# A transformer block on one core: DMA transposes and later transfers in the lead-in

## The chip, the cores and the metric

The kernel runs on one core of one Trainium2 chip. The metric is device time in microseconds (us) of one execution. Engines are called as in the profile: PE (matmuls; PEld is its weight load), DVE (vector), ACT (activations), POOL (GpSimd) and SP, which here only issues DMAs.

## The reference

A pre-norm transformer block in bf16, with 2048 rows of width 1024, 32 heads of 32 channels and an FFN width of 3584:

```
qkv = layernorm(x) @ wqkv                      # 1024 x 3072
o   = softmax(q k^T / sqrt(32)) v, per head
h   = x + o @ wo
out = h + gelu(layernorm(h) @ w1 + b1) @ w2 + b2
```

## The kernel before

**Order of the work.** The program is written as a graph of tasks, one per instruction or per small group, with an engine, a cost, a priority and the buffers that they read and write. `Graph.schedule` (L109) runs a list scheduler over it when the program is built and so fixes each engine's order; on the chip every engine works through its list in order and waits on semaphores. PE's choice among ready tasks is `pick_pe` (L1171): scores (kind "qk") first; then softmax times V ("pv") and row sums ("den") once enough rounds wait; then filler ("bg": projections, FFN), the lowest program number first. SP takes the lowest priority number first. Filler needs a PSUM bank: `slot()` (L518) hands out banks 6 and 7 alone, and the task that copies the result out gives the bank back. An attention job (one block of 256 queries of one head group) holds one of these banks from its first pv to the copies L866 and L873 in `finish`. Banks 0 to 5 hold scores, as three units of two banks.

**Attention.** A head group is 4 heads, 128 channels. A job has 8 rounds of 256 keys. A round is 8 score matmuls (`qk`, L784), two exponentials on ACT (L795, written to one of NR = 9 PT slots, and in the lead-in also to the extra slots PX that lie over buffers not yet in use), 8 pv matmuls (L821), an addition of the two key halves on DVE (L836, three buffers PS) and 4 matmuls with ones for the row sums (L850).

**Lead-in** (L1015 to L1087). The sixteen x tiles (128 rows each) are loaded into 8 buffers `xrb`. `lead_norm(hc)` (L1031) normalises two tiles into `xb` (4 buffers; statistics L598 and L613 on DVE, roots on POOL) and transposes both by 8 PE matmuls each (L619) into a shared bank, from which ACT (tiles 0 to 3) or DVE (the others, L628) copies to `xnT`. Each half `hc` of 256 rows then gives K of group 0 (`proj_half`, copied out by L758), the first three also Q, and three jobs (NLJ = 3) of group 0 start their score rounds on these halves: 24 rounds in all. V of a single head group (`proj_v1`, copied out by L740) comes from whole or strip matmuls: `mm(..., narrow)` makes either one 128-wide matmul (L549, L552) or four matmuls of 32 output rows (L546). `merge_tiles` (L210) turns runs of strip tasks back into whole ones where they stand alone or fill 3 us. The jobs' pv may start only when `gate`, the last copy of group 0's V, is done. After the lead-in come, for each group g, its Q and K projections (`proj`, copied out by L669), V, and the attention of query blocks 0 and 1, with 2 too for g = 1 and 2; the later query blocks run beside output projection and FFN. For those, `xnT` of rows 512 to 2047 is copied to DRAM (`xd`, three DMAs of 1 MB) in `lead_norm` and read back at about 258 us. Weights of groups 1 and up are loaded by `rest_w`, all after the load of x tile 15. In the FFN stage `ln2` transposes by DMA (L575) on SP's queue.

Of the kernel before, what the change touches and what calls it, by code (L numbers as in the profile page):

```python
# [12 lines left out]
P = 128  # L13
# [315 lines left out]
def build_kernel(nc, A_x, A_wqkv, A_wo, B_w1, B_b1, B_w2, B_b2, out):  # L329
# [98 lines left out]
    NXB = 4  # L428
# [106 lines left out]
    def drop(t, bank):  # L535
        if isinstance(bank, Slot):
            t.rel = bank

    def mm(bank, lhsT, rhs, start, stop, reads, narrow, cols=(0, 512), after=()):

        c0, c1 = cols
        occ = MM * (c1 - c0) / 512.0 + 0.0026
        if narrow:
            fns = []
            for j in range(4):
                fns.append(lambda p, j=j: p.matmul(psum[32 * j:32 * j + 32, bi(bank), c0:c1], lhsT[:, 32 * j:32 * j + 32], rhs,  # L546
                                                   start=start, stop=stop, tile_position=(0, 32 * j), skip_group_check=True))
            t = pe(fns, occ, reads=reads, writes=[bb(bank)], mode="col", after=after)
            t.whole = lambda p: p.matmul(psum[:, bi(bank), c0:c1], lhsT, rhs, start=start, stop=stop,  # L549
                                         skip_group_check=True)  # L550
# [99 lines left out]
    def proj(which, g, tc, bank, evac, direct=False):  # L650

        blk, c = divmod(which * D + g * P, 512)
        for dc in range(DC):
            mm(bank, Wall[blk][:, dc, c:c + P], xnT[:, tc, dc, :], dc == 0, dc == DC - 1,
               [B_W[blk][c // P]] + B_xnTt[tc], True)
        if which == 1:
            dst, wr = KT[:, g, 512 * tc:512 * tc + 512], B_KT[8 * g + 2 * tc:8 * g + 2 * tc + 2]
        elif direct:
            n = q_slot(0, g, 2)
            q_slots[1, g] = n + 1  # L660
            dst, wr = QT[:, n:n + 2, :].rearrange("p a c -> p (a c)"), B_QT[n:n + 2]
        else:
            s = cnt["sg"] % NSG
            cnt["sg"] += 1
            dst, wr = stg[:, s, :], [B_stg[s]]
        if evac == "act":
            t = act(lambda a: a.activation(dst, psum[:, bi(bank), :], ACT.Copy), 512, reads=[bb(bank)], writes=wr, prio=-1)
        else:
            t = dve(lambda v: v.tensor_copy(dst, psum[:, bi(bank), :]), c_dve_ps(512), reads=[bb(bank)], writes=wr)  # L669
# [92 lines left out]
    class Att:  # L762
# [8 lines left out]
        def qk(self, job, r, s=None):  # L771


            qb, g = job
            qs = q_slots[qb, g]
            us = [self.unit % self.n_units, (self.unit + 1) % self.n_units]
            self.unit += 2
            fns, banks = [], []
            for i in range(2):
                for h in range(4):  # L780
                    k0 = (2 * r + i) * P

                    def fn(p, i=i, h=h, k0=k0):
                        return p.matmul(psum[:, 2 * us[h // 2] + h % 2, 256 * i:256 * i + 256],  # L784
                                        KT[32 * h:32 * h + 32, g, k0:k0 + P], QT[32 * h:32 * h + 32, qs, :],
                                        start=True, stop=True, tile_position=(32 * h, 0))
                    fns.append(fn)
            for u in us:
                banks += [B_ps[2 * u], B_ps[2 * u + 1]]
            pe(fns, 0.222, reads=[B_KT[8 * g + r], B_QT[qs]], writes=banks, kind="qk", mode="row")  # L790
            if s is None:
                s = self.rounds % NR
                self.rounds += 1
            for k, u in enumerate(us):
                act(lambda a, u=u, k=k: a.activation(PTs[s][:, k, :, :], psum[:, 2 * u:2 * u + 2, :], ACT.Exp, bias=0.0, scale=SCALE),  # L795
                    1024, reads=[B_ps[2 * u], B_ps[2 * u + 1]], writes=[B_PTs[s][k]], kind="exp")
            return s
# [86 lines left out]
    pending = []  # L884

    def attention_round(job, r, lag=1):
        s = att.qk((job.qb, job.g), r)
        pending.append((job, r, s))
        attention_drain(lag)

# [155 lines left out]
    lead_rounds = []  # L1046
    lead_norm(0)
    for hc in range(8):
        ev = "act" if hc == 0 else "dve"
        if hc < NLJ:  # L1050
            proj_half(0, hc, slot(), ev)
        proj_half(1, hc, slot(), ev)
        if hc < 7:
            lead_norm(hc + 1)
        for k, r in [(k, hc) for k in range(min(hc, NLJ))] + ([(hc, r) for r in range(hc + 1)] if hc < NLJ else []):
            n = 8 * k + r
            s = NR + 15 if n == 0 else n - 1 if n < 9 else n
            lead_rounds.append((k, r, att.qk((k, 0), r, s)))
    att.rounds = 8
    hold = [t for t in gr.tasks if t.eng == E.DVE][-1:]  # L1060
    for c in range(4):
        proj_v1(4 * c, 0, 4, slot(), "dve", 0, True)
    gate = gr.tasks[-1]
    for k in range(NLJ):
        job = Job(k, 0, slot(2))
        for _, r, s in [x for x in lead_rounds if x[0] == k]:
            job.pv(r, s)
    pool_banks = {6: [t for t in gr.tasks if t.kind == "warm"][-1:], 7: []}
    lx = last_x[-1:]

    def rest_w(blk, c0, c1):
        load_w(blk, -3, c0, c1, after=lx)
# [84 lines left out]
    def ready_rounds(now):  # L1157
# [120 lines left out]
```

## Time and profile before

| | |
|---|---|
| median of 3 runs | 1090.35 us (1087.95 to 1093.55) |
| the profiled execution | 1091.97 us, its span 1090.2 us |
| mean granted PE clock | 0.994 |
| busy over the span | PE 96%, ACT 93%, DVE 69%, POOL 4%, DMA engines 54.1% |
| first 100 us, busy | PE 89.3, ACT 80.9, DVE 79.0 us |
| 100 to 200 us, busy | PE 99.1, ACT 100.0, DVE 63.5 us |
| 1000 to 1090.2 us, busy | PE 85.1, ACT 41.2, DVE 20.8 us |

The span is the time between the first and the last instruction that the profiler saw. A row of a timeline gives start, duration, engine, line, operation, output and inputs, and in brackets how long the engine was idle before it and which instruction released it. Times of stages are counted from the start of the span.

### The profile page before, as it was taken

Reading aid. Unit: us, or ns where it says so; the run is one execution under the profiler, and the core shown is the slowest. Engines: PE = TensorE matmul, PEld = TensorE weight load, DVE = VectorE, ACT = ScalarE, POOL = GpSimd, SP = SyncE. Lnnn points to the kernel's source line nnn. Section 1 sums busy time; section 2 is a strip of 40 time slices with the busy share of each in tenths; the row PEclk is TensorE's granted clock in tenths of the full one; section 3 lists DMA queues with packets and bytes.
Section 4 is the critical chain, followed back from the end, with each engine's and each line's share of the span. In section 5 each row is a group of like instructions: output and inputs, shape, how many; then the busy total and the mean of one; then the engine's idle time right before and its main releaser. Section 6 shows DMA issues by size and latency. Waiting matters only on the chain.

```text
span 1090.2 us, 41817 instructions
## 1 busy us (share of the span) xinstructions
PE 1045.6 (96%) x19048; PEld 609.6 (56%) x19107; DVE 755.9 (69%) x1453; ACT 1014.5 (93%) x1116; POOL 43.4 (4%) x110
## 2 busy tenths in 40 slices
PE   8989999998899999999999999999999999999998
PEld 6656555554344664574475457446545754474483
DVE  7886666666576896599489659948974967696401
ACT  4989999999999999999999999999999999999650
POOL 3200000000010001001000100100010000000100
PEclk9999999999999999999999999999999999899999
DMA  7640010008464667665685766567586656987370
GB/s 194 199 123 11 14 41 3 2 3 287 142 167 133 183 180 209 210 189 154 209 251 157 220 215 189 155 217 233 142 239 205 182 179 160 308 236 228 96 246 20
DMA packets 280146, 178.03 MB, mean 163 GB/s; under 512 B 42656, under 2 KB 274976, under 8 KB 279200
## 3 DMA queue, kind: packets, MB, share of 16 engines
q1 hardware_dynamic: 279968, 175.35, 54.1%
q8 instruction: 150, 2.46, 0.9%
q14 instruction: 28, 0.23, 0.1%
HBM read 161.16 MB, written 10.49 MB: 157 GB/s over the span
## 4 chain that ended last, share of the span: by engine, by line
PE 54%; ACT 39%; DVE 5%; issue 1%; DMA 1%; SPq 0%; POOL 0%; POOLq 0%; DVEq 0%
ACT PT L795 35%; PE ps L549 18%; PE ps L546 12%; PE ps L784 8%; PE ps L821 6%; PE ps L552 5%; PE ps L850 3%; ACT PX L795 2%; DVE PS L836 2%; ACT uu L983 2%; DMA xrb<-in_A_x_dram 0%; DVE OD L866 0%; PE ps L1025 0%; SPq L570 0%; DVE OD L873 0%
## 5 line engine op out<-in xcount | busy, mean ns | idle before, releaser
L795 ACT ACTIVATE PT<-ps 128x1024 bf16<-128x1024 f32 x992 | 922.4, 1082 | 14.7 <-PE ps L784 14.3
L836 DVE TENSOR_TENSOR PS<-PT 128x1024 bf16<-128x1024 bf16 x434 | 286.6, 685 | 128.9 <-PE ps L850 68.1
L784 PE MATMUL ps<-QT,KT 32*128 32x256 bf16 x4096 | 205.3, 274 | 10.7 <-ACT PT L795 5.4
L821 PE MATMUL ps<-PT,V 128*32 128x256 bf16 x3968 | 174.4, 274 | 2.8 <-ACT PT L795 2.8
L784 PEld LDWEIGHTS ps<-QT,KT 32*128 32x128 bf16 x4096 | 61.2, 92 | 166.3 <-ACT PT L795 134.8
L850 PE MATMUL ps<-PS,ones 128*32 128x256 bf16 x1792 | 124.6, 275 | 4.8 <-DVE PS L836 4.0
L821 PEld LDWEIGHTS ps<-PT,V 128*32 128x32 bf16 x3968 | 102.1, 97 | 29.4 <-issue 6.8
L549 PE MATMUL ps<-hnT,a_w1r 128*128 128x256 bf16 x949 | 116.5, 274 | 1.1 <-DVE gT L961 0.5
L549 PEld LDWEIGHTS ps<-hnT,a_w1r 128*128 128x128 bf16 x949 | 87.9, 98 | 25.8 <-issue 14.5
L546 PE MATMUL ps<-a_w2r,gT 128*32 128x512 bf16 x1372 | 98.3, 381 | 0.4 <-DVE hch L1007 0.2
L549 PE MATMUL ps<-a_w2r,gT 128*128 128x512 bf16 x382 | 93.8, 380 | 4.2 <-issue 2.9
L546 PE MATMUL ps<-hnT,a_w1r 128*32 128x256 bf16 x2476 | 88.9, 274 | 4.0 <-issue 1.6
L961 DVE TENSOR_TENSOR gT<-ps,b1f 128x512 bf16<-128x512 f32 x98 | 67.2, 686 | 17.5 <-PE ps L546 9.3
L546 PEld LDWEIGHTS ps<-hnT,a_w1r 128*32 128x32 bf16 x2476 | 60.4, 96 | 20.6 <-issue 16.8
L1007 DVE SCALAR_TENSOR_TENSOR hch<-ps,hch 128x512 bf16<-128x512 f32 x32 | 21.9, 685 | 69.9 <-PE ps L552 47.1
L850 PEld LDWEIGHTS ps<-PS,ones 128*32 128x32 bf16 x1792 | 47.0, 96 | 30.7 <-DVE PS L836 14.2
L549 PEld LDWEIGHTS ps<-a_w2r,gT 128*128 128x128 bf16 x413 | 35.2, 98 | 47.4 <-issue 13.4
L549 PE MATMUL ps<-xnT,Wall 128*128 128x512 bf16 (+1 forms) x256 | 53.5, 344 | 4.5 <-DVE rr L876 2.8
L983 ACT ACTIVATE uu<-uu 128x1024 bf16<-128x1024 bf16 x49 | 53.9, 1108 | 0.0
L546 PEld LDWEIGHTS ps<-a_w2r,gT 128*32 128x32 bf16 x1372 | 30.0, 96 | 25.6 <-issue 14.0
L603 POOL CAST mvb<-mv 128x2 bf16<-128x2 f32 (+1 forms) x25 | 4.9, 201 | 987.2 <-DVE mv L600 987.2
L549 PE MATMUL ps<-Wall,xnT 128*128 128x128 bf16 (+1 forms) x443 | 43.9, 247 | 0.0
(89 smaller groups left out, 1007.9 us busy)
## 6 DMA issues: line engine op xcount, KB each, us to landing
a_w2r<-in_B_w_dram SPq DMA_DIRECT2D x105, 512.0 KB, 5.7
a_w1r<-in_B_w_dram SPq DMA_DIRECT2D x98, 512.0 KB, 4.4
a_w1r<-in_A_wo_dram SPq DMA_DIRECT2D x32, 512.0 KB, 4.2
b_w1r<-in_B_w_dram SPq DMA_DIRECT2D x14, 512.0 KB, 6.1
a_w1r<-in_A_wqkv_dram SPq DMA_DIRECT2D x11, 512.0 KB, 5.0
Wall<-in_A_wqkv_dram SPq DMA_DIRECT2D x17, 256.0 KB, 4.7
xrb<-in_A_x_dram SPq DMA_DIRECT2D x16, 256.0 KB, 4.0
hch<-in_A_x_dram SPq DMA_DIRECT2D x16, 256.0 KB, 5.2
```

The lines of the kernel that those rows point to most:

```text
L546: fns.append(lambda p, j=j: p.matmul(psum[32 * j:32 * j + 32, bi(bank), c0:c1], lhsT[:, 32 * j:32 * j + 32], rhs, start=start, stop=stop, ...
L549: t.whole = lambda p: p.matmul(psum[:, bi(bank), c0:c1], lhsT, rhs, start=start, stop=stop, skip_group_check=True)
L552: t = pe(lambda p: p.matmul(psum[:, bi(bank), c0:c1], lhsT, rhs, start=start, stop=stop), occ, reads=reads, writes=[bb(bank)], mode="full" ...
L603: pool(lambda g: g.tensor_copy(mvb[:, sl, :], mv_l[:, sl, :]), 0.25, reads=B_mv[sl], writes=B_mvb[sl], prio=prio)
L784: return p.matmul(psum[:, 2 * us[h // 2] + h % 2, 256 * i:256 * i + 256], KT[32 * h:32 * h + 32, g, k0:k0 + P], QT[32 * h:32 * h + 32, qs, :],
L795: act(lambda a, u=u, k=k: a.activation(PTs[s][:, k, :, :], psum[:, 2 * u:2 * u + 2, :], ACT.Exp, bias=0.0, scale=SCALE), 1024, reads=[B_ps ...
L821: fns.append(lambda p, i=i, h=h: p.matmul(psum[32 * h:32 * h + 32, bi(bank), 0:256], V[:, g, 2 * r + i, 32 * h:32 * h + 32], PTs[s][:, h / ...
L836: dve(lambda v: v.tensor_tensor(PS[:, n, :, :], pairs[:, :, 0:256], pairs[:, :, 256:512], ALU.add), c_dve(1024, 2), reads=B_PTs[s], writes ...
L850: fns.append(lambda p, h=h, rhs=rhs, i=i: p.matmul(psum[32 * h:32 * h + 32, bi(bank), 256:512], ones32[:, :], rhs, start=False, stop=last, ...
L961: t = dve(lambda v: v.tensor_tensor(g[:, fc:fc + 2, :], psum[:, bi(bank), :].rearrange("p (f c) -> p f c", f=2), b1f[:, fc:fc + 2].unsquee ...
L983: act(lambda a: a.activation(w, w, ACT.Tanh, bias=0.0, scale=KT2), 1024, reads=[B_uu[i]], writes=[B_uu[i]], prio=-1)
L1007: drop(dve(lambda v, hs=hs, bank=bank, half=half: v.scalar_tensor_tensor(hch[:, hs, c], psum[:, bi(bank), :], half, hch[:, hs, c], ALU.mul ...
```

## The change

- x tiles 10 to 15 are transposed by DMA (`dma_transpose`, from `xb` straight into `xnT`) instead of by PE, PSUM and a DVE copy.
- V of groups 0 and 1 is asked for as whole matmuls (`narrow` left at False).
- `gate` is now two tasks, the last K half of group 0 and the last V copy of group 0. All matmul groups that are started after K of group 1 (`late`) wait for it, where before only V of group 1 did.
- Group 1's weights wait for x tile 11 instead of 15; all later weights wait for the transpose of tile 15.
- The copies of `xnT` to DRAM stand in the program after the lead-in and group 1's weights; their priority is as before.
- A Q projection that goes through the staging buffer `stg` waits for a free one before its first matmul rather than before its copy.
- The lead-in's jobs are made earlier and handed to `qk`; the order of the program is otherwise the same.

```
 def mm(bank, lhsT, rhs, start, stop, reads, narrow, cols=(0, 512), after=()):
+    after = list(after) + (late if start else [])
...
 def proj(which, g, tc, bank, evac, direct=False):
+    o = B_stg[cnt["sg"] % NSG]
+    free = o.w + o.r if which == 0 and not direct else []
...
+               [B_W[blk][c // P]] + B_xnTt[tc], True, after=free if dc == 0 else ())
...
+LEAD_PE = 10
+last_t = []
...
     for tt in tts:
-        tr_tile(tt, slot(), "act" if tt in LEAD_ACT else "dve")
+        if tt < LEAD_PE:
+            tr_tile(tt, slot(), "act" if tt in LEAD_ACT else "dve")
+        else:
+            tc, t4 = divmod(tt, 4)
+            last_t[:] = [dma_transpose(xnT[:, tc, :, t4 * P:(t4 + 1) * P], xb[:, tt % NXB, :], P * 2048, [B_xb[tt % NXB]], [B_xnTt[tc][t4]], -4)]
...
-    if hc in (3, 5, 7):
-        tc = hc // 2
-        dma(xd[tc - 1], xnT[:, tc, :, :], P * 8192, reads=B_xnTt[tc], writes=[B_xd[tc - 1]], prio=1)
...
     proj_half(1, hc, slot(), ev)
+    lead_k = gr.tasks[-1]
...
 for c in range(4):
-    proj_v1(4 * c, 0, 4, slot(), "dve", 0, True)
-gate = gr.tasks[-1]
+    proj_v1(4 * c, 0, 4, slot(), "dve")
+gate = [lead_k, gr.tasks[-1]]
...
-lx = last_x[-1:]
+lx = last_x[3:4]
...
 rest_w(WK, P, 2 * P)
 rest_w(WQ, P, 2 * P)
 rest_w(WV, P, 4 * P)
+lx = last_t or last_x[-1:]
+for tc in range(1, 4):
+    dma(xd[tc - 1], xnT[:, tc, :, :], P * 8192, reads=B_xnTt[tc], writes=[B_xd[tc - 1]], prio=1)
...
     for tc in range(4):
         proj(1, g, tc, slot(), "dve")
+    late[:] = gate
     if g == 1:
         for c in range(4):
-            proj_v1(4 * c, 1, 4, slot(), "dve", 0, True, [gate])
+            proj_v1(4 * c, 1, 4, slot(), "dve")
...
-    if gate.done is None or gate.done > now + 1e-9:
+    if any(x.done is None or x.done > now + 1e-9 for x in gate):
```

More of the change, by code (lines that the diff above doesn't have):

```diff
@@ L537, in drop @@
             t.rel = bank
+    late = []
     def mm(bank, lhsT, rhs, start, stop, reads, narrow, cols=(0, 512), after=()):
+        after = list(after) + (late if start else [])
         c0, c1 = cols
@@ L652, in proj @@
         blk, c = divmod(which * D + g * P, 512)
+        o = B_stg[cnt["sg"] % NSG]
+        free = o.w + o.r if which == 0 and not direct else []
         for dc in range(DC):
             mm(bank, Wall[blk][:, dc, c:c + P], xnT[:, tc, dc, :], dc == 0, dc == DC - 1,
-               [B_W[blk][c // P]] + B_xnTt[tc], True)
+               [B_W[blk][c // P]] + B_xnTt[tc], True, after=free if dc == 0 else ())
         if which == 1:
@@ L771, in qk @@
         def qk(self, job, r, s=None):
-            qb, g = job
+            qb, g = job.qb, job.g
             qs = q_slots[qb, g]
@@ L886, in attention_round @@
     def attention_round(job, r, lag=1):
-        s = att.qk((job.qb, job.g), r)
+        s = att.qk(job, r)
         pending.append((job, r, s))
@@ L1038, in lead_norm @@
         for tt in tts:
-            tr_tile(tt, slot(), "act" if tt in LEAD_ACT else "dve")
+            if tt < LEAD_PE:
[3 more added lines that the diff above has]
+                last_t[:] = [dma_transpose(xnT[:, tc, :, t4 * P:(t4 + 1) * P], xb[:, tt % NXB, :], P * 2048, [B_xb[tt % NXB]], [B_xnTt[tc][t4]], -4)]
             if tt + 8 < NT:
                 last_x.append(x_tile(tt + 8, -4))
-        if hc in (3, 5, 7):
-            tc = hc // 2
-            dma(xd[tc - 1], xnT[:, tc, :, :], P * 8192, reads=B_xnTt[tc], writes=[B_xd[tc - 1]], prio=1)
     lead_rounds = []
+    lead_jobs = [Job(k, 0, slot(2)) for k in range(NLJ)]
     lead_norm(0)
@@ L1057, in build_kernel @@
             s = NR + 15 if n == 0 else n - 1 if n < 9 else n
-            lead_rounds.append((k, r, att.qk((k, 0), r, s)))
+            lead_rounds.append((k, r, att.qk(lead_jobs[k], r, s)))
     att.rounds = 8
@@ L1061, in build_kernel @@
     for c in range(4):
-        proj_v1(4 * c, 0, 4, slot(), "dve", 0, True)
-    gate = gr.tasks[-1]
+        proj_v1(4 * c, 0, 4, slot(), "dve")
+    gate = [lead_k, gr.tasks[-1]]
     for k in range(NLJ):
-        job = Job(k, 0, slot(2))
         for _, r, s in [x for x in lead_rounds if x[0] == k]:
-            job.pv(r, s)
+            lead_jobs[k].pv(r, s)
     pool_banks = {6: [t for t in gr.tasks if t.kind == "warm"][-1:], 7: []}
-    lx = last_x[-1:]
+    lx = last_x[3:4]
     def rest_w(blk, c0, c1):
-        load_w(blk, -3, c0, c1, after=lx)
+        load_w(blk, -3, c0, c1, after=list(lx))
     rest_w(WK, P, 2 * P)
```

## The prediction

> **What bounds the kernel now.** I read the span first, then its last stretch, then the stalls of the engine that carries it. The page's head and the chain that ended last:
>
> ```profile
> span 1090.2 us, 41817 instructions
> ...
> PE 1045.6 (96%) x19048; PEld 609.6 (56%) x19107; DVE 755.9 (69%) x1453; ACT 1014.5 (93%) x1116; POOL 43.4 (4%) x110
> ...
> PE 54%; ACT 39%; DVE 5%; issue 1%; DMA 1%; SPq 0%; POOL 0%; POOLq 0%; DVEq 0%
> ```
>
> PE and ACT are both near full, so the shares do not say which sets the end. The end does. ACT's exponentials (L795) run without a gap from 991.6 to 1021.8 us; what follows (last output projection, layer norm, FFN of the last 256 rows) depends on them and takes the remaining 68.3 us. PE's filler work is done by about 1015: in 1015 to 1020 PE is busy 3.84 of 5 us. So the end is the last exponential plus a fixed tail, and the last exponential comes as early as ACT has few holes. In the first 100 us the largest hole in ACT after its start is here (timeline of ACT; in brackets the idle time ahead of the row):
>
> ```profile
> 65.06 7.65 ACT L795 ACTIVATE PT<-ps 128x1024 bf16<-128x1024 f32 x8
> 76.51 3.77 ACT L795 ACTIVATE PT<-ps 128x1024 bf16<-128x1024 f32 x4 [3.80 <-PE ps L784]
> ```
>
> From 76.51 to 273.7 ACT then never waits; all its waits for scores from 80 to 1000 add to 7.5 us. The 3.80 us are the prize. Where they come from (timeline around 73 us):
>
> ```profile
> 72.09 0.44 DVE L866 STREAM_TRANSPOSE OD<-ps 128x256 f32<-128x256 f32 x1
> 72.46 0.39 DVE L873 COPY OD<-ps 128x256 f32<-128x256 f32 x1
> ...
> 72.90 1.41 PEld L549 LDWEIGHTS ps<-xnT,Wall 128*128 128x128 bf16 x8 [2.25 <-DVE OD L873]
> ...
> 75.11 0.65 DVE L669 CAST KT<-ps 128x512 bf16<-128x512 f32 x1
> ...
> 76.06 0.40 PE L784 MATMUL ps<-QT,KT 32*128 32x256 bf16 x8
> ```
>
> Read upwards: the score round that ACT waits for (QK, L784) needs K of head group 1, third chunk, copied out at 75.11. Its matmuls start at 72.9, because both shared PSUM banks (6 and 7) were held by the softmax-times-V jobs of group 0 until DVE's L866 and L873 emptied one. DVE was late there since 53.5 us: it ran the row-sum additions (L836), 0.62 us apart in a run of eleven from 63.70 to 70.4. And K's third chunk was not made before the jobs took the banks because until 53.5 DVE was full (9.88 of 10 us in 30 to 40, 9.01 in 40 to 50) and the two banks passed every transposed x tile too.
>
> **The change, part by part.**
>
> Six transposes of sixteen leave PE and, with their copies (twelve run on DVE), DVE (groups of the first 100 us; the bar parts busy us and mean ns from idle time):
>
> ```profile
> L619 PE MATMUL ps<-ident,xb 128*128 128x128 bf16 x128 | 9.7, 220 | 1.8 <-DVE xb L613 1.5 <-DVE KT L758 0.2
> ...
> L628 DVE COPY xnT<-ps 128x1024 bf16<-128x1024 bf16 x12 | 8.1, 681 | 1.5 <-PE ps L619 1.4
> ```
>
> DVE loses 6 x 0.68 = 4.1 us, PE 6 x 8 matmuls, 6/16 of 9.7 = 3.6 us, and banks 6 and 7 lose six tenancies of about 0.62 + 0.2 + 0.68 = 1.5 us, 9 us of their 2 x 16 from 36 to 52. ACT is not waiting there, so by itself this is worth nothing at once; it lets PE make K of group 1 earlier (8 matmuls of 512 columns, 0.22 us each, and one 0.68 us copy: about 2.5 us of a bank per chunk). The 9 us hold three such chunks, and the second and third are what came at 61.3 and 75.1.
>
> Six DMA transposes come in on SP's queue. None stands in the lead-in of before; the same shape does later (DMA issues; the last number is us to landing):
>
> ```profile
> hnT<-a_xb SPq DMA_TRANSPOSE x14, 3.7
> ```
>
> They take 1.24 to 3.2 us of SP to issue and land after 2.7 to 6.5 us. A tile normalised by DVE (L613) came through PE and DVE in 2 to 4 us before, so each pair is later by 0 to 5 us; I take the median, 3.7. What hides it is how early K halves of group 0 are. Counting QK rounds: half 5 (tiles 10, 11) is copied out by 40.97 and first needed by the 16th round at 48.01, half 6 by 49.92 for the 19th at 53.51, half 7 by 53.51 for the 22nd at 59.13: slack 7.0, 3.6 and 5.6 us. For half 6, xb is ready at 43.8 and 44.3; second issue at 45.2, landing 47.9 to 51.7, projection and copy 1.8 more: 49.7 to 53.5 against 53.3 needed. It fits but for the slowest row, and DVE's earlier relief (two copies, 1.4 us) moves xb forward. The layer norms of tiles 14 and 15 must wait until the DMAs of 10 and 11 have read the same xb buffers: issued by about 37.4, landed by 44 at worst, used at 48.6: hidden. Behind a transpose that waits on SP stand only copies of xnT and weights not needed before 100 us: x tiles 14 and 15 are issued at 23.55, before the first transpose can be.
>
> V whole instead of in four strips: on the chip nearly nothing. In the rows to 56 us all 128 matmuls of group 0's V were whole already; of group 1's, 90 were whole and 38 in strips, and 24 strips' worth took 1.45 us, 26 whole ones 1.56. Where a whole matmul now stands beside strip work, an extra change costs 0.1 to 0.2 us (each change from QK shows 0.21 as issue); at most some 8 rounds, 0.8 to 1.7 us of PE in a stretch where PE idles 1.4 to 1.5 of 6 us: hidden.
>
> Weights: group 1's three loads wait for x tile 11 instead of 15, so they leave near 20 us instead of 26.8; their first use is at 41.6: 0. The later ones wait for the last transpose (about 52 us); first use at 105: 0, and uncovered only if they came 50 us late. The 1 MB copies of xnT come behind them in the program's order; they are read at 258: 0.
>
> The gate for V jobs and for all later fillers now also asks for K half 7, which precedes group 0's V in any case. V's last part needs tiles 14 and 15: xnT 15 between 50.4 and 56.9 (the 49.6 of before, less up to 2.7 us, issue and landing), then 2 to 3 us: the gate opens at 52.5 to 59 against 56.05 now. I take 56. Behind it DVE has 0.7 to 1.4 us less to do, since one or two K copies are made sooner.
>
> Sum: K's third chunk stands before 72.7 and the hole closes: -3.80. The next thing late is K's fourth chunk (copied at 77.0 now), needed two rounds on, at 72.7 + 3.7 = 76.4; a bank is free by 72.9, or by 67, when the second job's last row-sum matmuls are issued (66.9), if DVE empties it at once: 0 to +0.7, I take 0. Further down nothing changes but the start. So the profiled execution (1091.97 us with 1090.2 of span) would fall to 1088.2; it lies 1.6 above the median of the runs shown, 1090.35, and from the median I get **1086.6**.
>
> **The rivals.** A difference under 0.5% (5.45 us, 1084.9 to 1095.8) is about what a measurement of this kernel can tell from none.
>
> A, the forecast: the hole closes, 1086.6, give or take 2.5 for a rest whose order is planned anew. 47%.
>
> B, the hole moves. Group 1's V jobs began at 84.94, just as the tenth round of group 1 needed the first of nine PT slots back. With no stall the tenth comes at 81.9; if group 1's V still waits for banks as now, ACT waits 84.9 - 81.5 = 3.4 there. Against it: that V needs only 1.6 us of PE per quarter and banks are free sooner. Time 1090.0. 20%.
>
> C, PE was the bound after all (54% of the chain): then 3.6 us of transposes and the hole's PE idle time (2.2 before 73.13) both count, beside the 1.2 us ACT waits near 274 to 277: up to 3.8 + 3.6 = 7.4, 1083.0. For it: PE is busy over 99% from 100 to 265. Against it: it idles 0.4 to 0.7 a round from 267 to 272. 18%.
>
> D, slower: PE runs in order, and a K half whose transposes land late blocks the QK rounds queued behind it. It decides from 7.1 us after normalising (half 6: 53.3 - 1.8 - 44.3). The rows give 0.9 + 2.7 to 0.9 + 6.5 = 7.4. A transpose issued behind a 1 MB xnT copy (landing 3.8 to 6.0 us) could come some 2.6 us past that; for three pairs 7.8 us, with the hole unmended: 1098. For it: copies of tiles 8 to 11 are ready just as tiles 12 and 13 are. Against it: four late pairs (at 513, 609, 704, 800 us) issue in 2.6 to 3.4 us. 15%.
>
> The Trainium skill points to D (VectorE: DVE Perf Modes, The three transpose paths, and its rules): it gives 390 ns on TensorE and 1309 ns by DMA for a 128 x 128 block, and says to use TensorE if PSUM will do. By its figure, taken as serial, a tile of eight blocks would need an estimated 10.5 us, past D's point; the trace does not bear this out, with 2.7 to 6.5 us for a whole tile. Its tiling page (TensorEngine Tiling (Array Packing), Tiling Modes) says a change of tiling mode drains the engine; the 0.21 us gaps agree, and V's extra changes speak mildly against the change.
>
> **How the numbers follow.** Likeliest: A, 1086.6. The range takes in A, B and most of C, and not D: 1082 to 1095. Faster by over 0.5%: most of C and a fifth of A, 0.27. Slower by over 0.5%: D, 0.15. Within: 0.58.
>
> **What would show it.** Right: DVE shows six L628 copies instead of twelve, PE 80 L619 matmuls there; K of group 1 has three chunks copied by 67; ACT has no idle time over 1 us between 23 and 100; the last exponential ends near 1018. Wrong: ACT waits for L784 at 42 to 60 with PE waiting on a DMA into xnT (D); a wait near 82 to 85 with PE at group 1's V (B); or the hole closed and the last exponential unmoved, with new waits from 270 on.

## The result, and the profile after

| | before | after |
|---|---|---|
| median of 22 runs each, on the same chip | 1092.95 us | 1089.55 us |
| ratio, 95% interval | | 0.9971 (0.9959 to 0.9983) |
| the profiled execution, its span | 1091.97, 1090.2 us | 1089.97, 1088.2 us |
| mean granted PE clock | 0.994 | 0.991 |
| first 100 us, busy | PE 89.3, ACT 80.9, DVE 79.0 us | PE 91.7, ACT 83.1, DVE 76.8 us |
| ACT's waits between 40 and 103 us | 3.80 us in one | 2.26 us in three |
| last exponential ends | 1021.87 us | 1020.17 us |

The change makes the kernel 0.29% faster. The medians lie 3.40 us apart where 3.75 was forecast from the 1090.35 us shown before; the kernel before is a little slower in the larger sample, so the time itself, 1089.55, is 3 us above the forecast and inside its range. Ratios, here and below, leave out three executions far slower than the rest of their kernel (1183, 1457 and 2033 us).

The head of the page after and its chain that ended last look as before; by them nothing has changed:

```profile
span 1088.2 us, 41494 instructions
...
PE 1048.0 (96%) x18886; PEld 607.6 (56%) x18945; DVE 751.6 (69%) x1447; ACT 1015.6 (93%) x1116; POOL 43.4 (4%) x110
...
PE 56%; ACT 35%; DVE 6%; issue 1%; DMA 1%; POOL 0%; SPq 0%; POOLq 0%; DVEq 0%
```

Line numbers moved: the exponentials are now L800, scores L789, pv L826, row sums L855 with their DVE additions L841, the two copies that empty a job's bank L871 and L878, K of the later groups L674, K halves of group 0 L763, V L745. The timeline of ACT answers to the one with the 3.80 us:

```profile
64.40 7.72 ACT L800 ACTIVATE PT<-ps 128x1024 bf16<-128x1024 f32 x8
73.20 9.48 ACT L800 ACTIVATE PT<-ps 128x1024 bf16<-128x1024 f32 x10 [1.08 <-PE ps L789]
83.39 12.99 ACT L800 ACTIVATE PT<-ps 128x1024 bf16<-128x1024 f32 x14 [0.71 <-PE ps L826]
```

The hole of 3.80 us is gone. In its place stand three waits: 1.08 us at 72.1 to 73.2 for scores, 0.71 us before 83.39 for a PT slot (pv frees it), and one of 0.47 us before 96.85. The transposes did leave (groups of the first 100 us):

```profile
L622 PE MATMUL ps<-ident,xb 128*128 128x128 bf16 x80 | 6.0, 220 | 0.6 <-DVE xb L616 0.4 <-DVE KT L763 0.2
...
L631 DVE COPY xnT<-ps 128x1024 bf16<-128x1024 bf16 x6 | 4.0, 672 | 0.6 <-PE ps L622 0.6
```

And K of group 1 is early. DVE's timeline, its copies of the first, third and fourth chunk, of K half 7 of group 0 and of that group's last V:

```profile
43.41 0.69 DVE L674 CAST KT<-ps 128x512 bf16<-128x512 f32 x1
...
49.19 0.69 DVE L674 CAST KT<-ps 128x512 bf16<-128x512 f32 x1 [0.56 <-PE ps L552]
...
56.03 0.42 DVE L763 CAST KT<-ps 128x256 bf16<-128x256 f32 x1 [3.24 <-PE ps L552]
58.30 0.69 DVE L745 CAST V<-ps 128x512 bf16<-128x512 f32 x1
59.40 0.69 DVE L674 CAST KT<-ps 128x512 bf16<-128x512 f32 x1 [0.41 <-PE ps L549]
```

The third chunk stands at 49.9 instead of 75.8. K half 7, whose two x tiles now come by DMA, is copied at 56.03 instead of 53.09, and the gate opens at 59.0 instead of 56.05. The row of K half 7 in the kernel before:

```profile
53.09 0.42 DVE L758 CAST KT<-ps 128x256 bf16<-128x256 f32 x1 [1.57 <-PE ps L549]
```

What makes the new wait of 1.08 us is seen on PE just before it, and in the windows of 2 us there (span, busy time and count of PE, PEld, DVE, ACT and POOL, then PE's granted clock, DMA share, GB/s):

```profile
69.24 0.40 PE L826 MATMUL ps<-PX,V 128*32 128x256 bf16 x8 [1.28 <-DVE OD L878]
...
72.54 0.61 PE L789 MATMUL ps<-QT,KT 32*128 32x256 bf16 x8
```

```profile
68.00:70.00 2.00, 0.76 (x16) 0.24 (x16) 2.00 (x8) 2.00 (x3) 0.00 (x0) 0.92 0.00 0
70.00:72.00 2.00, 2.00 (x44) 1.43 (x44) 1.80 (x5) 2.00 (x3) 0.00 (x0) 0.50 0.04 8
72.00:74.00 2.00, 2.00 (x45) 0.96 (x38) 1.50 (x3) 0.92 (x2) 0.00 (x0) 0.73 0.72 185
```

PE waited 1.28 us for L878, the copy that empties a job's bank; DVE had nine additions (L841, 63.01 to 68.5) ahead of it. PE was busy 0.76 of the 2 us from 68, and then its granted clock was 0.50 from 70 to 72: the 8 score matmuls took 0.57 to 0.61 us instead of 0.40, all the pv work ahead of them took longer too, and ACT ran out of scores. This profile does not tell what the wait for the bank and what the clock cost; in e5 below both are gone. The Trainium skill (TensorE: Matmul & The Clock Gate, What's actually happening) says that the PE clock is either full or half, set by how busy PE was in windows of about 3.4 us that run on freely. The 0.50 agrees; the same section of the Trainium skill asks for an idle window of that length, and here PE was never idle for longer than 1.28 us between 50 and 70 us.

A sum shows where the time is in a profiled execution: start of the first long row of exponentials, plus ACT's waits in the lead-in, plus its waits after 103 us, plus the rest (the exponentials themselves and gaps too small to list). Before: 22.91 + 3.80 + 7.46 + 987.7 = 1021.87. After: 22.42 + 2.26 + 6.70 + 988.8 = 1020.17. The last exponential comes 1.70 us sooner: 0.49 from the start, 1.54 from the lead-in, 0.76 from later waits, less 1.1 in the rest. What follows it takes 68.0 us (68.3 before).

### The profile page after: what moved, and what is told of

Same layout as the page of the kernel before. It is cut to its first block, busy times and chain, and to the rows that moved or that the text cites. A ratio compares the mean times of both kernels' runs of the same rounds, so it can differ in the third digit from the quotient of the medians.

```text
span 1088.2 us, 41494 instructions
## 1 busy us (share of the span) xinstructions
PE 1048.0 (96%) x18886; PEld 607.6 (56%) x18945; DVE 751.6 (69%) x1447; ACT 1015.6 (93%) x1116; POOL 43.4 (4%) x110
## 4 chain that ended last, share of the span: by engine, by line
PE 56%; ACT 35%; DVE 6%; issue 1%; DMA 1%; POOL 0%; SPq 0%; POOLq 0%; DVEq 0%
ACT PT L800 32%; PE ps L552 19%; PE ps L549 12%; PE ps L789 9%; PE ps L826 6%; PE ps L555 6%; PE ps L855 4%; ACT PX L800 2%; DVE PS L841 2%; ACT uu L988 2%; DMA q_scratch<-lq 1%; DVE OD L871 0%; DVE st L601 0%; DMA xrb<-in_A_x_dram 0%; DVE OD L878 0%
## 5 line engine op out<-in xcount | busy, mean ns | idle before, releaser
L800 ACT ACTIVATE PT<-ps 128x1024 bf16<-128x1024 f32 x992 | 922.6, 1075 | 12.4 <-PE ps L789 11.2
L841 DVE TENSOR_TENSOR PS<-PT 128x1024 bf16<-128x1024 bf16 x434 | 286.5, 685 | 124.3 <-PE ps L855 65.5
L789 PE MATMUL ps<-QT,KT 32*128 32x256 bf16 x4096 | 205.1, 274 | 8.1 <-ACT PT L800 5.4
L826 PE MATMUL ps<-PT,V 128*32 128x256 bf16 x3968 | 175.6, 274 | 3.8 <-ACT PT L800 2.7
L789 PEld LDWEIGHTS ps<-QT,KT 32*128 32x128 bf16 x4096 | 60.9, 92 | 163.5 <-ACT PT L800 130.9
L855 PE MATMUL ps<-PS,ones 128*32 128x256 bf16 x1792 | 125.9, 276 | 3.8 <-DVE PS L841 2.9
L826 PEld LDWEIGHTS ps<-PT,V 128*32 128x32 bf16 x3968 | 101.9, 97 | 31.1 <-issue 7.9
L855 PEld LDWEIGHTS ps<-PS,ones 128*32 128x32 bf16 x1792 | 47.5, 97 | 30.0 <-DVE PS L841 12.9
L871 DVE STREAM_TRANSPOSE OD<-ps 128x256 f32<-128x256 f32 x64 | 28.6, 447 | 15.6 <-PE ps L826 9.2
```

The costliest lines, as they stand in the source:

```text
L826: fns.append(lambda p, i=i, h=h: p.matmul(psum[32 * h:32 * h + 32, bi(bank), 0:256], V[:, g, 2 * r + i, 32 * h:32 * h + 32], PTs[s][:, h / ...
L841: dve(lambda v: v.tensor_tensor(PS[:, n, :, :], pairs[:, :, 0:256], pairs[:, :, 256:512], ALU.add), c_dve(1024, 2), reads=B_PTs[s], writes ...
L855: fns.append(lambda p, h=h, rhs=rhs, i=i: p.matmul(psum[32 * h:32 * h + 32, bi(bank), 256:512], ones32[:, :], rhs, start=False, stop=last, ...
L871: t = dve(lambda v: v.transpose(OD[:, o, 1, :], psum[:, bi(bank), 256:512]), 0.36, reads=[self.B_O, self.B_D], writes=B_D, prio=-1)
```

## The experiments

Every kernel was compared with the kernel before on the same chip, over 12 runs (10 for e16, 6 for e25 and e57). K7 is the time at which DVE copies K half 7 of group 0 out, K1.3 and K1.4 are the third and fourth K chunk of group 1, all from one profiled execution, as are ACT's waits from 40 to 103 us. The first long row of exponentials starts between 21.7 and 23.2 us in these executions, so times of two kernels less than 1.5 us apart say little.

| kernel | ratio to before (95%) | K7 | K1.3 | K1.4 | waits |
|---|---|---|---|---|---|
| before | 1 | 53.09 | 75.11 | 77.03 | 3.80 |
| after | 0.9971 (0.9959 to 0.9983) | 56.03 | 49.19 | 59.40 | 2.26 |
| e1: before + DMA transposes | 1.0032 (1.0011 to 1.0053) | 59.47 | 52.33 | 62.77 | 11.69 |
| e13: e1 + whole V | 1.0036 (1.0018 to 1.0054) | 61.92 | 53.88 | 65.22 | 6.67 |
| e14: e13 + gate on fillers | 0.9969 (0.9953 to 0.9986) | 56.10 | 52.64 | 59.78 | 1.39 |
| e16: e13 + transfers moved | 0.9951 (0.9933 to 0.9970) | 58.25 | 48.99 | 61.14 | 3.25 |
| e12: after, transfers as before | 0.9963 (0.9947 to 0.9979) | 56.34 | 52.87 | 60.02 | 2.82 |
| e4: after, strips and old gate | 0.9964 (0.9945 to 0.9983) | 55.89 | 48.67 | 60.86 | 4.17 |
| e2: after, all transposes on PE | 0.9971 (0.9949 to 0.9994) | 54.50 | 64.38 | 76.70 | 3.38 |
| e11: before + whole V + gates | 0.9980 (0.9961 to 0.9999) | 53.69 | 63.57 | 75.90 | 3.39 |
| e18: before + whole V | 0.9989 (0.9971 to 1.0007) | 54.09 | 63.97 | 76.29 | 3.45 |
| e17: before + gate on fillers | 0.9978 (0.9961 to 0.9994) | 52.67 | 76.12 | 79.38 | 6.57 |
| e5: after + bank first | 0.9938 (0.9919 to 0.9958) | 55.97 | 49.14 | 59.34 | 0 |
| e25: e2 + bank first | 0.9925 (0.9903 to 0.9947) | 54.34 | 64.22 | 72.52 | 1.76 |
| e57: e5, four tiles by DMA | 0.9931 (0.9907 to 0.9955) | 53.52 | 49.91 | 60.14 | 0 |
| e6: before + bank first | 1.0004 (0.9985 to 1.0024) | 52.29 | 73.68 | 77.08 | 4.86 |

The table also shows how far one profile goes: e4 and e17 have more waiting in their profiled execution than the kernel before and are yet faster over their runs; the profiled execution of e2 (1093.67 us) is near the slowest of its runs (median 1088.33), that of e25 (1082.74) the fastest of its six (median 1085.28). A profile tells the mechanism; the ratio tells what it is worth.

**e1, the DMA transposes alone.**

```
 for tt in tts:
-    tr_tile(tt, slot(), "act" if tt in LEAD_ACT else "dve")
+    if tt < 10:
+        tr_tile(tt, slot(), "act" if tt in LEAD_ACT else "dve")
+    else:
+        tc, t4 = divmod(tt, 4)
+        dma_transpose(xnT[:, tc, :, t4 * P:(t4 + 1) * P], xb[:, tt % NXB, :], P * 2048, [B_xb[tt % NXB]], [B_xnTt[tc][t4]], -4)
```

> The kernel before with one part of the change: tiles 10 to 15 transposed by DMA; V, gate, weights and copies as before. Theory (the transposes' banks and DVE time are what closes the hole): K of group 1, third chunk, is copied out before 60 us instead of 75.1, the hole of 3.80 us at 72.7 is gone and ACT's waits for scores from 40 to 100 us add to under 1.5 us, so 2 to 4 us faster than before. Rival (the unchanged gate lets other filler take banks 6 and 7 ahead of V and the V jobs, and late halves of K block PE): the K chunks are early all the same, but waits of 3 us or more stand elsewhere between 40 and 90 us, and the time is that of before within 1 us.

Slower, 1.0032, which neither the theory nor its rival had. K of group 1 is early, as the forecast wanted, and ACT waits 11.7 us all the same, the longest times 3.14 us to 83.87 and 3.87 us to 92.90. The first has an odd cause on PE, in the middle of a job's pv matmuls:

```profile
79.79 0.28 PE L821 MATMUL ps<-PX,V 128*32 128x256 bf16 x4
83.09 0.29 PE L821 MATMUL ps<-PX,V 128*32 128x256 bf16 x4 [3.01 <-issue]
```

For 3.01 us PE waited for nothing that the profile shows. The other 1.30 us of this kind stand in the strips of group 1's V.

**e13, and V as whole matmuls.** Is it the strips, with four instructions for one?

```
-    proj_v1(4 * c, 0, 4, slot(), "dve", 0, True)
+    proj_v1(4 * c, 0, 4, slot(), "dve")
...
-            proj_v1(4 * c, 1, 4, slot(), "dve", 0, True, [gate])
+            proj_v1(4 * c, 1, 4, slot(), "dve", 0, False, [gate])
```

> The kernel before with two parts of the change: tiles 10 to 15 transposed by DMA, and V of groups 0 and 1 as whole matmuls. With the DMA transposes alone PE stood still for 3.01 us at 80 to 83 and 1.30 us at 91, both times ended by issue and both among V matmuls in strips (four instructions for one), while the DMA engines were full. Theory (four times as many instructions cannot be brought in fast enough there): no PE idle time over 1 us ended by issue between 60 and 100, ACT's waits between 40 and 100 fall from 11.7 us to under 6, time 1089 to 1091. Rival (the transfers alone or the new order make the stall, whatever V's form): PE idle times of 1 to 3 us ended by issue stay, ACT's waits stay over 9 us, time 1094 to 1096.

Half of each. From 60 to 100 us no idle time of PE over 0.2 us ended by issue is left, and ACT's waits fall from 11.7 to 6.7 us; but the time stays, 1.0036. So taking the stall away gained nothing. Of what is left, the two longest waits of ACT are 2.48 us ending at 62.94 and 2.50 us ending at 89.50, for a PT slot. The first of them, PE before it, and DVE beside it:

```profile
59.62 0.39 PE L546 MATMUL ps<-xnT,Wall 128*32 128x512 bf16 x4
...
60.81 1.06 PE L546 MATMUL ps<-xnT,Wall 128*32 128x256 bf16 x32 [0.58 <-DVE stg L669]
62.49 0.40 PE L784 MATMUL ps<-QT,KT 32*128 32x256 bf16 x8 [0.62 <-DVE KT L758]
```

```profile
57.35 0.69 DVE L740 CAST V<-ps 128x512 bf16<-128x512 f32 x1 [2.78 <-PE ps L552]
60.07 0.69 DVE L669 CAST stg<-ps 128x512 bf16<-128x512 f32 x1 [2.03 <-PE ps L546]
61.92 0.42 DVE L758 CAST KT<-ps 128x256 bf16<-128x256 f32 x1 [1.16 <-PE ps L546]
```

Read from below: the scores at 62.49 wait for K half 7, copied at 61.92. Its matmuls (the row of 32 strips at 60.81) wait for a bank, which the copy into `stg` at 60.07 gives back: a Q projection of group 1, filler that no score needs soon, had the bank, and the other had gone to the first job's pv when the gate opened with the V copy at 57.35. That V copy needs tiles 14 and 15 too, so their transposes had landed by then. The DMA transposes make K half 7 late enough to meet fillers at the banks, and there it loses some 4 to 5 us (by e14 below). Who gets the bank was settled when the program was built, by the scheduler's order.

**e14, and the gate on fillers.** One edit more than e13:

```
+    late = []
 def mm(bank, lhsT, rhs, start, stop, reads, narrow, cols=(0, 512), after=()):
+    after = list(after) + (late if start else [])
...
+        late[:] = [lead_k, gate]
         if g == 1:
```

> The kernel before with tiles 10 to 15 transposed by DMA, V of groups 0 and 1 whole, and one edit more: matmul groups started after K of group 1 wait for the last K half and the last V copy of group 0. Without that edit (DMA transposes and whole V alone) a Q projection of group 1 took a shared bank at 57, K half 7 of group 0 got its bank 0.6 us after that projection's copy, was copied out at 61.92 and cost ACT a wait of 2.48 us; time 1.0036 of before. Theory (the gate on fillers is what pays for the DMA transposes, since K half 7 is late and needs a bank at once): K half 7 copied out at 56 to 57, no ACT wait over 1 us from 45 to 65, 1089 to 1090.5. Rival (the other parts of the change, which this kernel lacks, make the difference): K half 7 at 60 or later, 1094 to 1096.

The theory holds. The ratio goes from 1.0036 to 0.9969, the intervals far apart, and K half 7 is copied 5.8 us sooner, of which 1.2 us is only the earlier start of this execution (21.99 against 23.22). The wait at 62.94 is gone, and that for a PT slot falls to 1.09 us:

```profile
56.10 0.43 DVE L761 CAST KT<-ps 128x256 bf16<-128x256 f32 x1 [2.77 <-PE ps L552]
58.38 0.68 DVE L743 CAST V<-ps 128x512 bf16<-128x512 f32 x1
```

**e16, the transfers instead of the gate.** The other edits of e13 stay, fillers are not held back:

```
-    lx = last_x[-1:]
+    lx = last_x[3:4]
...
     rest_w(WV, P, 4 * P)
+    lx = last_t or last_x[-1:]
+    for tc in range(1, 4):
+        dma(xd[tc - 1], xnT[:, tc, :, :], P * 8192, reads=B_xnTt[tc], writes=[B_xd[tc - 1]], prio=1)
```

(and the copies are taken out of `lead_norm`.)

> The kernel before with tiles 10 to 15 transposed by DMA, V whole, and the change's transfers (group 1's weights after x tile 11, later weights after the last transpose, copies of transposed x later in the program); gate as before, fillers not held back. Theory (earlier weights of group 1 bring the fillers, Q of group 1 among them, ahead of the stretch where K halves 6 and 7 need the banks, and so do the same as the gate on fillers; the kernel with strips and the old gate showed Q copied at 52.16 and K half 7 at 55.89): K half 7 by 57, 1088 to 1090.5. Rival (transfers are worth nothing, as forecast): K half 7 at 60 or later, 1094 to 1096.

Faster than expected, 0.9951. With group 1's weights there earlier, its Q is copied out of the bank at 52.65, where e13 had it at 60.07:

```profile
52.65 0.69 DVE L669 CAST stg<-ps 128x512 bf16<-128x512 f32 x1 [2.97 <-PE ps L549]
54.48 0.42 DVE L758 CAST KT<-ps 128x256 bf16<-128x256 f32 x1 [1.14 <-PE ps L549]
...
58.25 0.42 DVE L758 CAST KT<-ps 128x256 bf16<-128x256 f32 x1 [2.62 <-PE ps L546]
```

It now delays K half 6 (54.48; ACT waits 1.95 us to 55.50), but K half 7 loses less. K half 7 is a little later than the theory asked, 58.25 for "by 57"; the rival's 60 is not reached. So either of two parts of the change undoes what the DMA transposes cost. Neither e14 nor e16 has the staging buffer's earlier wait or the jobs made earlier, so these two parts, which were not run alone, are not needed for it.

**e12, after without the transfers.** Group 1's weights wait for x tile 15 again, and the 1 MB copies stand in `lead_norm` (the diff of e16, backwards).

> The changed kernel with weights and copies as they were: group 1's weights wait for x tile 15, the later ones too, and the 1 MB copies of transposed x stand in the lead-in. Theory (the moved transfers are worth nothing, as forecast): 1088 to 1090, K of group 1 copied out by 50 for three chunks, gate near 59. Rival (the copies stand ahead of the transposes on the queue and hold them up): the last V copy of group 0 at 61 or later, QK rounds of group 0 late, ACT waits of 2 us or more between 45 and 65, time 1092 to 1095.

As the theory said in time, 0.9963, and in the gate, 59.3; no wait reaches 2 us. The third chunk, at 52.87, is later than its "by 50". With the copies ahead of them the transposes do take longer (1.23 to 2.57 us to issue and 3.1 to 6.0 us to land, where the change has 1.23 to 1.41 and 3.1 to 3.5), but K half 7 at 56.34 is as early as in the change. With the gate on fillers the moved transfers are worth nothing that was measured; without it (e13 to e16) they are worth 0.85%.

**e4, after with strips and the old gate.**

```
-    proj_v1(4 * c, 0, 4, slot(), "dve")
+    proj_v1(4 * c, 0, 4, slot(), "dve", 0, True)
-gate = [lead_k, gr.tasks[-1]]
+gate = [gr.tasks[-1]]
...
-        late[:] = gate
...
-                proj_v1(4 * c, 1, 4, slot(), "dve")
+                proj_v1(4 * c, 1, 4, slot(), "dve", 0, True, gate)
```

> The changed kernel with V in strips and with the old gate (last V copy alone, asked of group 1's V alone); DMA transposes and transfer order as in the change. Theory: the hole stays closed, ACT's waits from 40 to 100 us are within 1 us of the changed kernel's 2.3, same time as the changed kernel within 1.5 us. Rival (gate and whole V carry the gain): waits of 3.5 us or more there, and the time of before.

0.9964, the same as after: with the transfers early, neither whole V nor the gate is needed. The time is the theory's; the waits, 4.17 us, are the rival's, 1.71 us of them at K half 6, as in e16. It fits e16, which it joins to the change from the other side.

**e2, after with all sixteen transposes on PE.**

```
-LEAD_PE = 10
+LEAD_PE = 16
```

> The changed kernel with all sixteen tiles transposed by PE again; the rest of the change stays (whole V, two-part gate, earlier group 1 weights, later other weights). Theory: without the relief K's third chunk is made after the V jobs have taken the banks, a hole of 2 us or more near 72 to 78 is back, and the time is within 1 us of before. Rival (earlier weights or the gate close the hole): no ACT wait over 1.2 us from 40 to 100, and 2 to 4 us faster than before.

The theory has the wait, the rival the time: 1.93 us of the hole are back (to 77.88, and 1.45 us to 84.93 for a PT slot), and the ratio is that of six tiles by DMA, 0.9971. The DMA transposes add nothing to the rest that these runs can tell.

**e11, e18 and e17, the parts that need no DMA transpose.** e11 has whole V, the gate in two parts and the gate on fillers; e18 has whole V alone (the diff of e13, on the kernel before), e17 the gate on fillers alone (the diff of e14, likewise).

> The kernel before with the other half of the change: V of groups 0 and 1 whole, the gate in two parts, and all matmul groups after K of group 1 waiting for it; every transpose on PE, weights and copies as before. Theory (the gate and whole V carry most of the gain, since the changed kernel with all transposes on PE was as fast as with six by DMA): 1088 to 1089, ACT's waits between 40 and 100 about 2 to 3.5 us. Rival (the gain comes from the weights and copies moved later, which this kernel lacks): 1091, with one wait of 3 to 4 us near 73 to 77 as before.

> The kernel before with one edit: V of groups 0 and 1 as whole matmuls. Theory (whole V alone brings the second and third K chunks of group 1 forward, since its matmul groups are shorter and give the banks back sooner; the gate on fillers matters only where K halves come late by DMA): as whole V with the gate, K chunks of group 1 copied near 46, 57, 64 and 76, ACT waits near 77 and 84 of 1.9 and 1.5 us, 0.998 of before. Rival (the gate on fillers did it): as before, chunks at 48, 61, 75 and 77, one wait of 3.8 us, 1.000.

> The kernel before with one edit: matmul groups started after K of group 1 wait for the last K half and the last V copy of group 0; V in strips, all transposes on PE. Theory (with all transposes on PE K half 7 is early, and nothing competes with it for a bank, so the gate holds back nothing that would have run): as before, 1.000, one wait of 3.8 us. Rival (the gate brings group 1's K chunks forward): chunks as with whole V and the gate, 46, 57, 64 and 76, 0.998.

e11 gives 0.9980, and two waits of 1.94 and 1.45 us in place of the one that its rival had; its median of 1090.93 stood beside a before of 1093.31. In e18 the chunks and waits are those of e11 within half a us:

```profile
57.24 0.69 DVE L669 CAST KT<-ps 128x512 bf16<-128x512 f32 x1 [0.19 <-PE ps L546]
63.97 0.64 DVE L669 CAST KT<-ps 128x512 bf16<-128x512 f32 x1
76.29 0.65 DVE L669 CAST KT<-ps 128x512 bf16<-128x512 f32 x1
```

```profile
77.54 5.60 ACT L795 ACTIVATE PT<-ps 128x1024 bf16<-128x1024 f32 x6 [2.00 <-PE ps L784]
84.59 18.68 ACT L795 ACTIVATE PT<-ps 128x1024 bf16<-128x1024 f32 x20 [1.45 <-PE ps L821]
```

Whole V alone brings the third chunk from 75 to 64. The hole then goes on to the fourth chunk, still late at 76.29 because DVE empties the bank late, and to the PT ring: 3.45 us of waits for 3.80, and 0.9989, not to be told from 1. In e17 the first two chunks are those of the kernel before, the third and fourth come 1.0 and 2.4 us later, and the hole is there, but larger, 6.57 us. The row behind it, first in the kernel before and then in e17:

```profile
73.13 3.00 PE L549 MATMUL ps<-xnT,Wall 128*128 128x512 bf16 x13 [2.19 <-DVE rr L876]
```

```profile
72.89 5.59 PE L552 MATMUL ps<-xnT,Wall 128*128 128x512 bf16 x13 [2.36 <-DVE rr L879]
```

The same thirteen matmuls (K's third and part of its fourth chunk, which PE has ahead of the scores) after about the same idle time take 3.00 us at a granted clock of 1.00 and 5.59 us at 0.50. The windows of e17 from 72 to 76 read 0.50; those of the kernel before 1.00. So in these two executions the hole cost 3.8 us at full clock and 6.6 us at half. e17's ratio, 0.9978, is a little below the 1.000 expected, with 1 just outside its interval; what makes that is open.

**e5, e25, e57 and e6: the bank first.** After's 1.08 us and e18's 2.00 us both hang on DVE's additions ahead of the copies that empty a job's bank. One edit, on two lines of `finish`, for the jobs of group 0 in the lead-in:

```
-    writes=B_D, prio=-1)
+    writes=B_D, prio=-3 if g == 0 and qb < 3 else -1)
...
-    writes=B_O, prio=-1)
+    writes=B_O, prio=-3 if g == 0 and qb < 3 else -1)
```

e5 is after with it, e25 is e2 with it (all transposes on PE), e57 is e5 with tiles 14 and 15 on PE, and e6 is the kernel before with it.

> The changed kernel with one new edit: DVE takes the two copies that empty a group 0 job's bank (L871, L878) ahead of the row-sum additions (L841). Theory on the 1.08 us wait at 72.1 in the changed kernel: PE idles from 67 to 69.2 because a bank is not emptied while DVE adds, its clock then falls to half for some 3 us, and the scores come late; with the copies first, the clock stays at 1.0 from 60 to 80 us, that wait is under 0.3 us, and the time is 1 to 2 us under the changed kernel's, 4 to 5 under before. Rival (the clock falls or the scores are late for another reason, such as too few V rounds ready): a wait over 0.8 us at 66 to 76 stays and the time is the changed kernel's.

> The changed kernel with all sixteen transposes on PE and, on DVE, the two copies that end a job of group 0 in the lead-in ahead of the row-sum additions. Theory (what matters is that DVE empties the shared banks at once; six transposes more on PE and DVE cost little): ACT waits under 1 us in all between 40 and 100, time 1086 to 1087.5, as with six transposes by DMA and the same priority (1086.4). Rival (DVE and the banks are too full with all transposes on PE): K of group 1, third chunk, copied out after 70 again and a wait of 1.5 us or more near 73 to 78, time 1088 to 1090.

> The changed kernel with only tiles 10 to 13 transposed by DMA (14 and 15 on PE) and the two copies that end a job ahead of the row-sum additions on DVE. Theory (with the banks emptied at once, the number of DMA transposes matters little): ACT's waits between 40 and 100 under 2 us, 1085 to 1087, between six by DMA (1086.4) and none (1085.3). Rival (DMA transposes of the last two tiles are what opens the gate late, at 59; with them on PE it opens at 56 to 57 and all later work comes 2 us earlier): 1083 to 1085.

> The kernel before with one edit: on DVE the two copies that end a job of group 0 in the lead-in go ahead of the row-sum additions. No part of the change. Theory (the wait of 3.80 us hung on DVE emptying the shared bank late; the transposes had little to do with it): the wait to 76.51 falls under 1 us, the last exponential ends 3 to 4 us earlier, 1086 to 1088. Rival (K of group 1, third chunk, stays late because banks and DVE are full with transposes until 53): a wait of 2 us or more stays between 70 and 80, 1089 to 1091.

In e5 ACT does not wait once between 25 and 269 us. Its long row, and the first job's copy on DVE:

```profile
64.34 204.44 ACT L800 ACTIVATE PT<-ps 128x1024 bf16<-128x1024 f32 x222
```

```profile
63.55 0.44 DVE L871 STREAM_TRANSPOSE OD<-ps 128x256 f32<-128x256 f32 x1
```

The two copies of the first job stand at 63.6 to 64.3 and those of the second at 68.4 to 69.2, where after has both pairs one behind the other at 68.4 and 69.1. The clock stays at 1.00 from 60 to 80. The ratio is 0.9938. e25 and e57 are as fast, 0.9925 and 0.9931, their intervals over each other: with the banks emptied at once these runs show no difference between none, four and six tiles by DMA. In e57 the gate opens at 56.5, as its rival had it, but the ratio is no lower than e25's; its median, 1084.94, at the border of both forecasts, stood beside a before of 1093.77. e25 has the lowest ratio seen and needs no DMA transpose; it keeps one wait, where the theory had under 1 us in all:

```profile
68.71 0.44 DVE L871 STREAM_TRANSPOSE OD<-ps 128x256 f32<-128x256 f32 x1
...
72.52 0.69 DVE L674 CAST KT<-ps 128x512 bf16<-128x512 f32 x1
```

```profile
83.05 27.87 ACT L800 ACTIVATE PT<-ps 128x1024 bf16<-128x1024 f32 x30 [1.76 <-PE ps L826]
```

e6 was a miss: the same edit on the kernel before gives 1.0004. DVE empties the second job's bank at 67.84 instead of 72.9, PE fills it with K's third chunk by 70.3, and then:

```profile
73.11 3.18 PE L546 MATMUL ps<-xnT,Wall 128*32 128x512 bf16 x28 [1.36 <-DVE OD L873]
76.22 0.50 PE L784 MATMUL ps<-QT,KT 32*128 32x256 bf16 x8
```

DVE copies the third chunk at 73.68 only, after more additions, and by then PE is in the strips of the fourth chunk, which stand before the scores in its order and run at a clock of 0.50 from 74 to 76. ACT waits 4.86 us to 76.77. In these kernels emptying the bank early helped only where K's chunks had come forward already.

## Why the prediction came out as it did

**Direction and size came out about right, the reason did not.** 3.40 us between the medians stand against the 3.75 forecast. That they are so close is luck: the hole, forecast at 3.80 and alone in the sum, gave 1.54 us net in the profiled executions, and the part that was to bring the gain brings none that was measured. (With 22 runs of each a measurement tells 0.12% from nothing, finer than the 0.5% that the chances went by.) The step that failed is the one that names the prize's owner: "Six transposes of sixteen leave PE and, with their copies, DVE", whose freed bank time was to make K of group 1 early. The counts and busy times of that step came out (six copies, 4.0 us; 80 matmuls, 6.0 us), and K's third chunk was early. But the DMA transposes alone make the kernel slower (e1, 1.0032), and all the rest of the change without them is as fast (e2, 0.9971). K's third chunk comes to 64 by whole V alone (e18), soon enough for the round that waited; but the fourth chunk is then late (76.29), and whole V alone is not told from no gain.

**"Weights: 0" and the gate at nothing.** Both were priced as if K half 7 had no rival for its bank. The working counted its slack against landing times and did not ask who else could take a bank while it was late. So these two terms went wrong: against e13, the gate on fillers is worth 0.67% (e14) and the transfers 0.85% (e16). Once one of the two is there, the other is worth nothing that was measured (e12, e4).

**The DMA transposes as hidden.** They were issued in 1.23 to 1.41 us each and landed after 3.1 to 3.5 us, at the short end of the rows used (1.24 to 3.2, 2.7 to 6.5). The gate opened at 59.0, the late end of the 52.5 to 59 given; 56 was the value taken. In the change this was hidden, since no ACT wait stands between 23 and 72 us. Without the gate or the transfers it was not (2.48 us in e13).

**Rival D was real, in another place.** It was priced at 1098 for late K halves blocking the scores behind them. e13, at 1096.4, is that case in 2.48 of its 6.67 us of waits, but the K half waited for a bank, not for a landing, and the point from which it decides (7.1 us after normalising) has no part in it. In e1, at 1095.4, the wait at K half 7 is 1.07 of 11.69 us.

**V whole at nothing.** In time this holds: e1 to e13 no gain, e18 not to be told from 1. The mechanism was missed: the third chunk of K moves by 11 us, the second by 4.

**The sum's "next late".** Taken as K's fourth chunk, 0 to 0.7 us. In the change that chunk was early (59.40); instead DVE's late emptying of a bank cost 1.08 us with the clock at half, the PT ring 0.71 us (rival B in small: it had 3.4), and a third wait 0.47 us. The lead-in's gain was therefore 1.54 us net and not 3.80 in the profiled execution, and the end of the last exponential 1020.17 and not near 1018. Of the signs that were named, the copies, the matmuls and the three chunks came out; that ACT has no idle time over 1 us did not. Where the fourth chunk was the next late thing (e2, e11, e18), it cost 1.9 to 2.0 us.

**The cause of the hole.** The prediction's chain, banks held until DVE's L866 and L873, additions ahead of those, is shown by e5 and e25: with that alone mended, the waits went from 2.26 us to none and from 3.38 to 1.76. That it is half of the cause is shown by e6: K's chunks must also be forward. **Rival C**, PE as the bound, finds no support: e25 has all transposes on PE and is no slower than e5, which has ten of the sixteen there.

**Open.** The ratios of after, e2, e4, e11, e12 and e14 lie within 0.2% of each other, and nothing here orders them. Nor is it shown which part gives e2 its gain, the DMA transposes left out: whole V (0.9989) and the gate on fillers (0.9978) alone are not told from e11 or e2, and the moved transfers were not run alone on the kernel before. How the losses of e1 and e13 come about is shown only in part. Their runs have a mean granted clock of 0.987, those of the kernel before and of e14 0.992 and 0.994. By the 0.82 us for 0.001 given below, an estimated 4 us of e1's and e13's time and 5 to 6 us of the step from e13 to e14 go with the clock. Whether the waits of these kernels lower it is not shown. Against the clock as the whole cause stand e16 (0.988) and e4 (0.989), both faster than before. Nor is it settled why e16 is ahead of e14 while its profiled execution waits more, nor what stopped PE for 3.01 us in e1. It stood among pv matmuls, behind strips of V, fell together with busy DMA engines (mean share 1.00 from 80 to 83) and was gone without the strips; but the 1.30 us came at a DMA share of 0.12.

## What to carry to other kernels

When a step is made later on purpose, ask not only whether it lands in time but who takes its buffers while it is late: here one condition on fillers was worth 0.67% where the six transposes it protected gave nothing that was measured. When a change has several parts, run each by itself before crediting the one that it is named for. And look at the engine that gives a scarce buffer back: two short copies put ahead of additions that the scores did not wait for gave about as much again as the whole change (0.9938 against 0.9971), once the work that wanted the buffer was ready.

## What the runs showed of the hardware

- **The half clock comes without a long idle time, and not always.** After fell to 0.50 with PE busy 2.1 of the 4 us from 66 to 70 and never idle for over 1.3 us; e17 was at 0.50 behind an idle time of 2.36 us and the kernel before at 1.00 behind one of 2.19 us, with the same work. The clock time lost over the span, from windows of 5 us, came near multiples of 1.7 us (5.1 before, 8.6 after, 17.0 in e1), which is 3.4 us at half clock.
- **About two fifths of the spread between runs of one kernel goes with the mean granted clock.** Over 113 runs of the kernel before (those that e1 to e57 were compared with, one of 1457 us left out), 0.001 of clock less goes with 0.82 us more (give or take 0.19 at 95%), and the standard deviation falls from 2.4 to 1.8 us when this is taken out: median 1096.4 us at 0.988 and 0.989 (13 runs), 1091.0 at 0.994 and 0.995 (25 runs).
- **A DMA transpose of a 128 x 1024 tile** took 1.23 to 1.41 us to issue and landed after 3.1 to 3.5 us, 3.3 in the median, in the changed kernel. In e13, where a 1 MB copy was issued ahead of the first four and of the last two, it took 1.23 to 2.46 us and landed after 3.1 to 5.9 us, 4.4 in the median.
